# Moving sums to VectorE and block copies to ScalarE, decoding weights in slices of 768, and re-pricing the hand-written order of a delta-rule plus channel-mixer kernel

## The chip, the core and the metric

The kernel runs on one core of a Trainium2 chip. The metric is the device time of one execution in microseconds (us). Engines are called PE (TensorE, matrix products), DVE (VectorE), ACT (ScalarE), POOL (GpSimd) and SP (the engine that only issues DMAs here). PEld is PE's weight load.

## What is computed

Four batches, eight heads, 768 time steps, 48 dimensions per head. First a delta-rule recurrence runs over time, then its output `x` (768 x 384 per batch) goes through a mixer with a low-rank product over the sequence and two dense layers over the channels. The weights arrive as 64-bit floats, everything else as fp32.

```
k_n = k / (norm(k) + 1e-6)
for t in range(S):
    y[t]  = q[t] @ state
    v_old = state^T k_n[t]
    state = state + beta[t] * outer(k_n[t], v[t] - v_old)
x  = y as (B, S, 384)
u  = x + (x^T @ U @ V)^T                    # U 768x32, V 32x768
out = u + relu(u @ w_ch1) @ w_ch2           # w_ch1 384x1536, w_ch2 1536x384
```

## The kernel before

**Recurrence.** Time is cut into chunks of 64, six chunks make a unit, two units make a batch, so there are eight units n = 0..7 and two SBUF slots that they share in turn. For each unit `grams` transposes k and q on PE (L380), copies them on ACT (L395) and forms the products k·k and q·k (L407, masked on DVE at L431). `blocks` then inverts the triangular systems: DVE transposes the diagonal blocks of 32 (L481), runs a forward substitution of pairs of instructions `prod` (L490) and `xt` (L496), and transposes back (L503). With `split = 2` (units 0 to 3) a block of 32 is solved as two blocks of 16 in 15 steps, and `joins` puts the halves together with small PE products (L534, L551) and extra DVE work (L513, L559). With `split = 1` (units 4 to 7) there are 31 longer steps. The joined blocks of 64 are made by L581 to L602, the results negated and copied by L610 (ACT) and L613 (DVE), and the diagonal blocks are copied into the slot by L624 (POOL, 48 times) and L627 (ACT, 16 times); POOL also clears blocks (L631). `prepare` makes two more products (L704, L715), copied by L723 (ACT) and L728 (DVE). `recur` steps through the twelve chunks of a batch: PE products L753, L781, L668, L682, with the DVE instructions `z` (L766) and `s` (L791) between them and copies of the output into `X` on ACT (L652).

**Mixer.** `front` (L903, L917, L925) makes `ut`, the transposed u, for 256 time steps. `wide` first multiplies by w_ch1 (L990, 72 PE records, then the relu on ACT, L946), and then by w_ch2 (L1026, 84 records, added into `X` on DVE, L975). I call these two halves "wide" and "narrow"; there are twelve of each, three per batch. The narrow half uses seven products of half size in place of eight, which needs sums of hidden activations (`add_up` L962, `last_sum` L969, both on POOL) and of weights (`sums`, L815, POOL, eight instructions).

**Weights.** `load_weights` decodes 64-bit floats on the fly: a slice of 384 columns is loaded into `wide` through POOL's DMA queue (L835), and five DVE instructions (L852, L861, L867, L872, L880) with one of ACT (L857) turn it into fp32. There are 27 slices: U, two of V, twelve of w_ch1, twelve of w_ch2. The first wide half needs all of w_ch1, the first narrow half all of w_ch2 and the weight sums.

**Order.** Nothing is scheduled at run time. Each part is a generator that yields the engine and price of its next operation; `run` keeps one clock for each engine, and picks the next operation by place in a priority list and by modelled time. The order found in this way is the program's order on each engine[...]. A price in an `op(...)` call is therefore no time on the chip: it only moves instructions. `SWITCH` and `HOLD` are the model's charges for changing PE's kind of work and for holding back. For example:

```
yield op("pool", 1.2)
nc.gpsimd.tensor_tensor(out=w[:, to], in0=w[:, a], in1=w[:, c], op=ALU.subtract)
```

Of the kernel before, what the change touches and what calls it, by code (L numbers as in the profile page):

```python
# [26 lines left out]
def kernel(  # L27
# [36 lines left out]
    HD = DM // 2  # L64

# [17 lines left out]
    clock = dict(pe=0.8, dve=0.8, act=0.8, pool=0.8, sp=0.8)  # L83
# [4 lines left out]
    SWITCH, HOLD = 0.15, 0.15  # L88
# [8 lines left out]
    def op(engine, cost, mode=None, take=None, give=(), lat=None, rush=None, words=0):  # L97
        return dict(e=engine, cost=cost, mode=mode, take=take, give=give, words=words + 2,
                    rush=bool(give) if rush is None else rush, lat=LAT[engine] if lat is None else lat)
# [26 lines left out]
    def run():  # L126
        while waits:
            some = {}
            for i in sorted(waits):
                while isinstance(waits.get(i), list) and all(x in done for x in waits[i]):  # L130
                    at = max([0.0] + [done[x] for x in waits[i]])
                    if at > ready[i]:
                        last[i] = None
                    advance(i, None, max(at, ready[i]))
                s = waits.get(i)
                if s is None or isinstance(s, list):
                    continue
                e, was = s["e"], last.get(i)
                at = max(was[1] if was and was[0] == e else ready[i], clock[e])
                if s["take"]:  # L140
                    banks, of = places(s)
                    if not of:
                        continue
                    at = max(at, min(banks[y] for y in of))
                if s["mode"] and s["mode"] != state["mode"]:
                    at += SWITCH
                some.setdefault(e, []).append((at, i))
# [28 lines left out]
            state["now"] = clock[s["e"]] = at + cost  # L176
            if s["mode"]:
                state["mode"] = s["mode"]
# [87 lines left out]
    def load(n, name, halves):  # L266
# [13 lines left out]
        for g in halves:  # L280
            for s in range(1, 4, 2) if name == "z" else range(4):
                to = dict(k=s, q=s, v=s % 2 * 2 + s // 2, z=s // 2)[name]
                yield op(e, 0.65)
                queue.dma_start(
                    out=t[half(1 - g if name == "z" else g), :, to, 0:D],
                    in_=src[b, 4 * g + s, hf * UC * L : (hf + 1) * UC * L, :].rearrange(
                        "(c t) d -> t c d", t=L
                    ),
                )
                after = landing(384)  # L290
                if name == "z" or s % 2:
                    emitted((name, n, g, s // 2), after)
# [4 lines left out]
    def load_beta(u):  # L297
        beta_sb = X.rearrange("p a b d -> p (a b d)")[0 : 4 * B, 0 : 2 * S].rearrange(
            "p (g s) -> p g s", g=2
        )  # L300
        if u == 0:
            for g in range(2):
                yield op("pool", 0.6)
                nc.gpsimd.dma_start(out=beta_sb[:, g], in_=beta[:, 4 * g : 4 * g + 4])
            yield op("pool", 0.0, lat=landing(64, 0.1))
        else:
            yield need(("gram", 0))
# [30 lines left out]
    def norms(n):  # L338
# [9 lines left out]
        yield op("dve", 0.9)  # L348
# [24 lines left out]
    def grams(n, i):  # L373
# [26 lines left out]
        def products(j, i):  # L400
            yield need(("laid", n)) if i else []
            x = yield op("pe", 0.75, "Q", take="pair", words=96)
# [25 lines left out]
            else:  # L428
                for par in range(2):
                    yield op("dve", dve(384), give=[("pair", x)] if par else (), rush=n >= NU)  # L430
# [28 lines left out]
    def blocks(n):  # L459
        _, _, pg, _, _, _, diag, _ = units[n]  # L460
        split = 2 if n in (0, 1, 2, 3) else 1
# [18 lines left out]
        yield op("dve", dve(BK * BK))  # L480
# [3 lines left out]
        yield op("dve", dve(1024 // split))  # L484
        nc.vector.tensor_tensor(out=gb, in0=gb, in1=by, op=ALU.mult)
        for j in range(size - 1):
            m, w = j + 1, size - 1 - j
            yield op("dve", 2 * dve(split * m * w) - 0.08)
# [13 lines left out]
        yield op("dve", dve(BK * BK))  # L502
# [17 lines left out]
        def joins(r):  # L520
# [53 lines left out]
            for c in range(UC):  # L574
                if c % 3 == 0:
                    got = yield op("pe", 0.23, "J", take=None if c else "pair", words=48)
# [13 lines left out]
            for c in range(UC):  # L590
                if c % 3 == 0:
                    got = yield op("pe", 0.23, "J", take=None if c else "pair", words=48)
# [12 lines left out]
            for g in range(2):  # L605
                rows = quarter(2 * g)
                to = pg[rows, r, :, :, BK:L]
                if g == 0:
                    yield op("act", act(384), rush=True)
                    nc.scalar.mul(to, p_v[rows], -1.0)  # L610
                else:
                    yield op("dve", dve(384), give=[("pair", x)])
                    nc.vector.tensor_scalar_mul(to, p_v[rows], -1.0)  # L613
            emitted(("upper", n, r), 0.1)

        def diagonals(r):
            at = slice(12 * r, 12 * r + 12)
            yield need(("whole", n, r))
            for i in range(4):
                a = BK * (i % 2)  # L620
                to, of = heads(pg[quarter(i)])[:, at, a : a + BK], zc[quarter(i), at]
                if i < 2 or r == 0:
                    yield op("pool", 0.5)
                    nc.gpsimd.tensor_copy(out=to, in_=of)  # L624
                else:
                    yield op("act", act(384))
                    nc.scalar.copy(to, of)  # L627
# [12 lines left out]
    def recur(b):  # L640
# [19 lines left out]
        def outputs(c, s_old):  # L660
# [3 lines left out]
            y = yield op("pe", 0.35, "Q", take="pair", words=32)  # L664
            p_y = pair(y)[:, :, 0 : 2 * D]
            if c > 0:
# [11 lines left out]
                yield op("pe", 0.35, "Q", words=32)  # L678
# [16 lines left out]
        def prepare(n, h):  # L695
# [4 lines left out]
            x = yield op("pe", 0.76, "Q", take="pair", words=96)  # L700
# [10 lines left out]
            y = yield op("pe", 0.76, "Q", take="pair", words=96)  # L711
# [15 lines left out]
            yield op("dve", dve(576), give=[("pair", y)])  # L727
            nc.vector.tensor_copy(  # L728
# [10 lines left out]
        for c in range(NC):  # L739
# [9 lines left out]
            else:  # L749
                xb = yield op("pe", 0.35, "Q", take="pair", words=32)  # L750
# [24 lines left out]
            if c < NC - 1:  # L775
                yield need(("y1", b, c)) if c else []
                xs = yield op("pe", 0.35, "Q", take="pair", words=32)
# [18 lines left out]
    WIDE = 384  # L796

    def weight_slices():
        yield u_sb.rearrange("p c r -> p (c r)"), moe_U, NB
        for s0 in range(0, S, WIDE):  # L800
            yield v_sb[:, s0 : s0 + WIDE], moe_V[:, s0 : s0 + WIDE], None
        for f in (0, 2, 1, 3):
            for t in range(KT):
                at = slice(f * WIDE, (f + 1) * WIDE)
                yield w1_sb[:, t, at], moe_w_ch1[t * 128 : (t + 1) * 128, at], None
        for f in range(HF):
            yield w2_sb[:, 0:4:3, f], moe_w_ch2[f * 128 : (f + 1) * 128, :], None
            at = slice((HF + f) * 128, (HF + f + 1) * 128)
            yield w2_sb[:, 1:3, f], moe_w_ch2[at, :], None

    def sums(f):
        w = w2_sb[:, :, f : f + 3]
        for to, a, c in ((4, 3, 0), (5, 2, 4), (6, 1, 5), (3, 2, 3)):
            yield op("pool", 1.2)
            nc.gpsimd.tensor_tensor(out=w[:, to], in0=w[:, a], in1=w[:, c], op=ALU.subtract)  # L815
        emitted(("sums", f), 0.2)

    def load_weights():
        landed = {}
        slices = list(weight_slices())  # L820

        def start(i):
            dst, src, groups = slices[i]
            n = WIDE if len(dst.shape) == 3 else dst.shape[1]
            wide = conv.tile([128, n, 2], I32, name="wide")
            src = src.bitcast(I32)
            to = wide.rearrange("p n two -> p (n two)")
            copies = 1 if groups else 128 // src.shape[0]
            if groups:
                to = to.rearrange("p (c r) -> p c r", c=groups)  # L830
                src = src.rearrange("(c p) r -> p c r", c=groups)
            for x in range(copies):
                yield op("pool", 0.55)
                at = slice(x * 128 // copies, (x + 1) * 128 // copies)
                nc.gpsimd.dma_start(out=to[at], in_=src)  # L835
            landed[i] = wide
            emitted(("wide", i), landing(128, 0.13) + 0.6)
# [3 lines left out]
        for i in range(len(slices)):  # L841
            dst = slices[i][0]
            n = WIDE if len(dst.shape) == 3 else dst.shape[1]
# [3 lines left out]
            yield op("dve", 0.36)  # L847
            wide = landed.pop(i)
            h, low = wide[:, :, 1], wide[:, :, 0].bitcast(U32)
            power = conv.tile([128, n], I32, name="power", bufs=1)  # L850
            upper = conv.tile([128, n], I32, name="upper", bufs=1)
# [4 lines left out]
            yield op("act", 0.62, lat=-0.62)  # L856
# [3 lines left out]
            yield op("dve", 0.36)  # L860
# [5 lines left out]
            yield op("dve", 0.57)  # L866
# [4 lines left out]
            yield op("dve", 0.57)  # L871
# [4 lines left out]
            yield op("dve", 0.57)  # L876
            power = power.bitcast(FP32)
            if len(dst.shape) == 3:
# [5 lines left out]
            if i >= 3 + KT * DFF // WIDE and (i - 3 - KT * DFF // WIDE) % 6 == 5:  # L884
                begin(sums((i - 3 - KT * DFF // WIDE) // 6 * 3), 21)
# [7 lines left out]
    def front(b, i):  # L893
        yield need(
            ("front", *before(b, i)), ("wide", *before(*before(b, i))),
            ("weights", 2), *[("x", b, c) for c in range(NC)],
# [17 lines left out]
        def block(c):  # L914
            o = yield op("pe", 0.72, "F", take="pair", words=4)
# [6 lines left out]
            o = yield op("pe", 0.38, "F", take="pair", words=6)  # L922
# [12 lines left out]

    def wide(b, i):
        yield need(("front", b, i), ("narrow", *before(b, i)))
        x, ut = X[:, b % 2], uts[b, i]
        if b == 0 and i == 0:
            state["slow"] = 1.0  # L940
            yield op("pe", 0.0, take=("pair", 3))
            free["mix"].update({0: state["now"], 1: state["now"]})
# [10 lines left out]
        def add_up(f0, fs):  # L953
            yield need(*[("h", b, i, x) for x in fs])
            at = slice(f0, f0 + 3)
            for to, a, c, how in (
# [4 lines left out]
                yield op("pool", 0.8)  # L961
                nc.gpsimd.tensor_tensor(out=to, in0=a, in1=c, op=how)  # L962
            emitted(("summed", b, i, f0), 0.1)

        def last_sum():
            yield need(("summed", b, i, 0), ("summed", b, i, 3), ("half", b, i, 1))
            yield op("pool", 1.5)
            a = part(1, 0, 0, HF)
            nc.gpsimd.tensor_tensor(out=a, in0=a, in1=S2, op=ALU.subtract)  # L969
# [13 lines left out]
        for y, fs in enumerate(((0, 1), (2, 6), (7, 8), (3, 4), (5, 9), (10, 11))):  # L983
            for f in fs:
                yield need(("weights", 2 + KT * ((0, 2, 1, 3).index(f // 3) + 1)))
# [48 lines left out]
    with tc.manual_schedule():  # L1034
# [16 lines left out]
        begin(load_weights(), 40)  # L1051
        for b in range(B):
# [36 lines left out]
```

## Time and profile before

| what | value |
|---|---|
| median of 3 runs | 751.82 us (751.59 to 757.63) |
| the profiled execution | 749.14 us, span 747.4 us |
| PE busy | 621.5 us (83%) |
| DVE busy | 396.9 us (53%), 928 instructions |
| ACT busy | 183.5 us (25%), 369 instructions |
| POOL busy | 208.9 us (28%), 265 instructions |
| mean granted TensorE clock | 0.881 |
| twelve wide halves (L990) on PE | 205.2 us |
| twelve narrow halves (L1026) on PE | 179.9 us |
| substitution (L490 and L496) on DVE | 150.5 us |
| sums of activations on POOL (L962, L969) | 94.8 us |
| sums of weights on POOL (L815) | 11.6 us, eight instructions |

The span is the trace's own length; the profiled execution's time is 1.7 us above it. A busy share is an average over stages that differ: up to about 200 us the recurrence of batches 0 and 1 and the decoding of weights fill DVE, and from about 560 us on only the mixer is left and PE is always busy. The profile's chain of waits is followed back from the last instruction, so it shows what set the end and not only what was busy.

### The profile page before, as it was taken

Reading aid. Unit: us, or ns where it says so; the run is one execution under the profiler, and the core shown is the slowest. Engines: PE = TensorE matmul, PEld = TensorE weight load, DVE = VectorE, ACT = ScalarE, POOL = GpSimd, SP = SyncE. Lnnn points to the kernel's source line nnn. Section 1 sums busy time; section 2 is a strip of 40 time slices with the busy share of each in tenths; the row PEclk is TensorE's granted clock in tenths of the full one; section 3 lists DMA queues with packets and bytes.
Section 4 is the critical chain, followed back from the end, with each engine's and each line's share of the span. In section 5 each row is a group of like instructions: output and inputs, shape, how many; then the busy total and the mean of one; then the engine's idle time right before and its main releaser. Section 6 shows DMA issues by size and latency. Waiting matters only on the chain.

```text
span 747.4 us, 25030 instructions
## 1 busy us (share of the span) xinstructions
PE 621.5 (83%) x11304; PEld 539.9 (72%) x11304; DVE 396.9 (53%) x928; ACT 183.5 (25%) x369; POOL 208.9 (28%) x265
## 2 busy tenths in 40 slices
PE   5567677956698897876799587799999999999998
PEld 4556665745587676755778586688888989989998
DVE  6998788999832269989227989821110110101001
ACT  3232346422112343211226211222112011120110
POOL 7443311355212111322301231330213131221412
PEclk9555569965689999879999787999999999999999
DMA  9603657412002243000324200000000000000000
GB/s 154 97 19 91 144 146 170 104 42 68 2 4 53 55 72 69 27 3 2 58 52 90 52 13 13 3 2 23 3 22 1 22 0 22 11 11 22 1 22 22
DMA packets 87051, 33.38 MB, mean 45 GB/s; under 512 B 81760, under 2 KB 84832, under 8 KB 86944
## 3 DMA queue, kind: packets, MB, share of 16 engines
q1 hardware_dynamic: 81856, 19.18, 13.5%
q0 software_dynamic: 3488, 12.29, 6.2%
q8 instruction: 89, 1.46, 0.8%
q10 hardware_dynamic: 1600, 0.30, 0.2%
q14 instruction: 18, 0.15, 0.1%
HBM read 27.03 MB, written 4.72 MB: 42 GB/s over the span
## 4 chain that ended last, share of the span: by engine, by line
PE 42%; DVE 20%; issue 2%; ACT 2%; DVEq 0%
PE P L990 18%; PE P L1026 17%; DVE prod L490 6%; DVE xt L496 6%; DVE zz L503 1%; PE P L917 1%; DVE slot L431 1%; PE P L781 1%; PE P L753 1%; PE P L925 1%; DVE gs L481 1%; DVE z L766 1%; ACT X L652 1%; DVE slot L420 1%; DVE X L921 1%
## 5 line engine op out<-in xcount | busy, mean ns | idle before, releaser
L990 PE MATMUL P<-ut,w_sb 128*128 128x256 f32 x864 | 205.2, 391 | 3.6 <-ACT hs L946 3.6
L990 PEld LDWEIGHTS P<-ut,w_sb 128*128 128x128 f32 x864 | 163.3, 194 | 26.7 <-ACT hs L946 4.0
L1026 PE MATMUL P<-w_sb,hs 128*128 128x192 f32 x720 | 128.2, 335 | 0.5 <-DVE X L975 0.5
L1026 PEld LDWEIGHTS P<-w_sb,hs 128*128 128x128 f32 x720 | 120.5, 195 | 3.8 <-issue 1.2
L975 DVE TENSOR_TENSOR X<-X,P 128x192 f32<-128x192 f32 x84 | 29.6, 353 | 157.3 <-PE P L1026 157.2
L946 ACT ACTIVATE hs<-P 128x512 f32<-128x512 f32 x72 | 42.8, 596 | 226.5 <-PE P L990 212.1
L962 POOL TENSOR_TENSOR S<-hs 128x384 f32<-128x384 f32 x24 | 24.3, 1011 | 264.7 <-ACT hs L946 264.7
L490 DVE TENSOR_TENSOR prod<-gs,xt 128x30 f32<-128x30 f32 (+20 forms) x184 | 77.5, 421 | 4.4
L496 DVE TENSOR_TENSOR xt<-xt,prod 128x30 f32<-128x30 f32 (+20 forms) x184 | 73.0, 397 | 6.3
L652 ACT COPY X<-P 64x192 f32<-64x192 f32 x96 | 30.1, 314 | 93.0 <-PE P L682 71.8
L1026 PE MATMUL P<-w_sb,S 128*128 128x192 f32 x288 | 51.7, 336 | 0.0
L1026 PEld LDWEIGHTS P<-w_sb,S 128*128 128x128 f32 x288 | 48.7, 196 | 0.5
L407 PE MATMUL P<-slot 48*64 48x64 f32 x1536 | 36.6, 260 | 10.9 <-DVE slot L613 6.3
L407 PEld LDWEIGHTS P<-slot 48*64 48x64 f32 x1536 | 32.9, 171 | 15.3 <-DVE slot L613 6.4
L380 PE MATMUL P<-ident,slot 128*128 128x128 f32 x192 | 31.9, 315 | 11.0 <-DMA slot<-in_k_dram 7.0
L921 DVE TENSOR_TENSOR X<-X,P 128x384 f32<-128x384 f32 x24 | 12.7, 547 | 46.5 <-PE P L917 46.1
L624 POOL COPY slot<-zz 32x384 f32<-32x384 f32 x48 | 24.6, 512 | 40.1 <-DVE zz L559 38.2
L380 PEld LDWEIGHTS P<-ident,slot 128*128 128x128 f32 x192 | 25.0, 160 | 14.7 <-issue 13.5
L969 POOL TENSOR_TENSOR hs<-hs,S 128x768 f32<-128x768 f32 x12 | 22.0, 1829 | 41.5 <-PE P L1026 41.5
L766 DVE TENSOR_TENSOR z<-slot,P 128x192 f32<-128x192 f32 x44 | 15.5, 353 | 31.1 <-PE P L753 30.0
L925 PE MATMUL P<-ident,X 128*128 128x128 f32 x72 | 13.5, 312 | 20.5 <-DVE X L921 20.3
L363 POOL TENSOR_TENSOR slot<-slot,norm_rows 128x1152 f32<-128x1152 f32 x8 | 18.8, 2349 | 40.2 <-DMA slot<-in_q_dram 28.1
(108 smaller groups left out, 857.3 us busy)
## 6 DMA issues: line engine op xcount, KB each, us to landing
wide<-in_moe_w_ch_dram POOLq DMA_DIRECT2D x24, 384.0 KB, 3.9
slot<-in_k_dram SPq DMA_DIRECT2D x84, 72.0 KB, 3.3
slot<-in_q_dram SPq DMA_DIRECT2D x64, 72.0 KB, 3.3
out_dram<-X SPq DMA_DIRECT2D x24, 192.0 KB, 1.8
slot<-in_v_dram SPq DMA_DIRECT2D x48, 72.0 KB, 2.5
slot<-in_v_dram POOLq DMA_DIRECT2D x16, 72.0 KB, 4.3
wide<-in_moe_V_dram POOLq DMA_DIRECT2D x8, 96.0 KB, 5.5
slot<-in_k_dram POOLq DMA_DIRECT2D x8, 72.0 KB, 6.4
```

What stands on the lines that cost most here:

```text
L380: nc.tensor.transpose(p_t[:, c // 3, c % 3], t[:, c, 2 * j : 2 * j + 2].rearrange("p s d -> p (s d)"), ident,)
L407: nc.tensor.matmul(p_g[half(g ^ (par * i)), par, c], kq[rows, c, j, 0, half(g)], kq[rows, c, j, i, half(g)], start=True, stop=True,)
L490: nc.vector.tensor_tensor(out=prod, in0=gb[:, :, j : j + 1, j + 1 :].to_broadcast([128, split, m, w]), in1=xb[:, :, 0:m, j : j + 1].to_bro ...
L496: nc.vector.tensor_tensor(out=xb[:, :, 0:m, j + 1 :], in0=xb[:, :, 0:m, j + 1 :], in1=prod, op=ALU.subtract,)
L624: nc.gpsimd.tensor_copy(out=to, in_=of)
L652: nc.scalar.copy(x[half(c % 2), c // 2, 4 * D * g : 4 * D * (g + 1)].rearrange("p (j r d) -> p r j d", r=2, d=D), states(p_y)[half(g)],)
L766: nc.vector.tensor_tensor(out=z.rearrange("p (r j) d -> p r (j d)", r=2), in0=vn[:, cu].rearrange("p (r j) d -> p r (j d)", r=2), in1=p_b, ...
L946: nc.scalar.activation(hs[:, fs[0] : fs[1] + 1 : fs[1] - fs[0]], p_f, ACTF.Relu)
L962: nc.gpsimd.tensor_tensor(out=to, in0=a, in1=c, op=how)
L975: nc.vector.tensor_tensor(out=to, in0=to, in1=p, op=ALU.add)
L990: nc.tensor.matmul(p_f[:, fs.index(f)], w1_sb[:, t, f * 128 : (f + 1) * 128], ut[:, t], start=(t == 0), stop=(t == KT - 1),)
L1026: nc.tensor.matmul(p_o, a[:, f], w2_sb[:, w, f], start=(first and f == 0), stop=(f == HF - 1), skip_group_check=True,)
```

## The change

Six things are done at once.

1. All sums leave POOL for DVE: `sums` (eight instructions of 128x576), `add_up` (72 of 128x384) and `last_sum` (12 of 128x768).
2. Block copies leave POOL and DVE for ACT: all 64 diagonal copies, both negated copies (L613), and the copy after the product L715 (L728).
3. Weights are decoded in slices of 768 columns: U, one slice of V, six of w_ch1, six of w_ch2. Their loads go through SP's queue (that of U stays on POOL's). Half of the buffers lie in `X[:, 1]`, batch 1's part of `X`, which is not needed yet; beta's staging moves from `X` to `hs` for that.
4. Only units 0 and 1 are solved in blocks of 16; units 2 and 3 now use 31 steps.
5. The order model gets a `port` clock, shared by POOL's operations and by the DVE operations with `port=True`, and many prices change. This alters the order on every engine.
6. Two PSUM banks are reserved for the mixer by a part of its own (`reserve`).

```
-    clock = dict(pe=0.8, dve=0.8, act=0.8, pool=0.8, sp=0.8)
+    clock = dict(port=0.0, pe=0.8, dve=0.8, act=0.8, pool=0.8, sp=0.8)
-    SWITCH, HOLD = 0.15, 0.15
+    SWITCH, HOLD = 0.18, 0.18
...
+                if s["port"]:
+                    at = max(at, clock["port"])
...
+            if s["port"]:
+                clock["port"] = at + cost
...
-        split = 2 if n in (0, 1, 2, 3) else 1
+        split = 2 if n in (0, 1) else 1
...
-                if g == 0:
-                    yield op("act", act(384), rush=True)
-                    nc.scalar.mul(to, p_v[rows], -1.0)
-                else:
-                    yield op("dve", dve(384), give=[("pair", x)])
-                    nc.vector.tensor_scalar_mul(to, p_v[rows], -1.0)
+                yield op("act", act(384), rush=True, give=[("pair", x)] if g else ())
+                nc.scalar.mul(to, p_v[rows], -1.0)
...
-                if i < 2 or r == 0:
-                    yield op("pool", 0.5)
-                    nc.gpsimd.tensor_copy(out=to, in_=of)
-                else:
-                    yield op("act", act(384))
-                    nc.scalar.copy(to, of)
+                yield op("act", act(384))
+                nc.scalar.copy(to, of)
...
-            yield op("dve", dve(576), give=[("pair", y)])
-            nc.vector.tensor_copy(
+            yield op("act", act(576), give=[("pair", y)])
+            nc.scalar.copy(
                 out=vn[:, cs[0] : cs[2] + 1].rearrange("p c (r j) d -> p r c (j d)", r=2),
...
-    WIDE = 384
+    WIDE = 768
...
-            yield op("pool", 1.2)
-            nc.gpsimd.tensor_tensor(out=w[:, to], in0=w[:, a], in1=w[:, c], op=ALU.subtract)
+            yield op("dve", dve(576), port=True)
+            nc.vector.tensor_tensor(out=w[:, to], in0=w[:, a], in1=w[:, c], op=ALU.subtract)
...
+        room = X.bitcast(I32).rearrange("p a b d -> p a (b d)")[:, 1]
+        wides = [room[:, 0 : 2 * WIDE], conv.tile([128, 2 * WIDE], I32, name="wide", bufs=1)]
+        uppers, powers = room[:, 2 * WIDE :], conv.tile([128, WIDE], I32, name="power", bufs=1)
...
+            e, queue = ("pool", nc.gpsimd) if i < 1 else ("sp", nc.sync)
+            for to, of in pieces:
+                yield op(e, 0.6, port=False)
+                queue.dma_start(out=to, in_=of)
...
+    def reserve():
+
+        yield [("x", 0, NC - 2)]
+        yield op("pe", 0.0, take=("pair", 3))
+        free["mix"].update({0: state["now"], 1: state["now"]})
+        emitted("mixing")
...
-                yield op("pool", 0.8)
-                nc.gpsimd.tensor_tensor(out=to, in0=a, in1=c, op=how)
+                yield op("dve", dve(384), port=True)
+                nc.vector.tensor_tensor(out=to, in0=a, in1=c, op=how)
...
-            yield op("pool", 1.5)
+            yield op("dve", dve(768), port=True)
             a = part(1, 0, 0, HF)
-            nc.gpsimd.tensor_tensor(out=a, in0=a, in1=S2, op=ALU.subtract)
+            nc.vector.tensor_tensor(out=a, in0=a, in1=S2, op=ALU.subtract)
```

## The prediction

> **What bounds the kernel now.** I read the page's slices first. The rows are tenths of busy time in forty slices of 18.7 us.
>
> ```profile
> PE   5567677956698897876799587799999999999998
> DVE  6998788999832269989227989821110110101001
> PEclk9555569965689999879999787999999999999999
> ```
>
> DVE is full in the first ten slices while PE is half idle at a low clock; from slice 30 on PE is full. The page gives averages, so I cut the span at the ends of the recurrences of batches 0 to 3, which the timeline of L682 shows at 117, 265.5, 393 and 562.3 us. Busy time by stretch, with count in brackets:
>
> ```profile
> core 0: us, PE busy (x) PEld busy (x) DVE busy (x) ACT busy (x) POOL busy (x), PEclk, DMA share, GB/s
> 0.00:117.00 117.00, 77.77 (x2812) 69.08 (x2816) 96.64 (x244) 41.05 (x85) 49.63 (x88) 0.64 0.56 110
> 117.00:158.00 41.00, 33.39 (x379) 26.26 (x370) 36.97 (x76) 18.04 (x32) 14.61 (x15) 0.92 0.53 120
> 158.00:199.00 41.00, 21.43 (x890) 18.57 (x888) 38.87 (x80) 9.24 (x19) 18.69 (x22) 0.58 0.12 39
> 265.50:393.00 127.50, 102.88 (x2175) 86.19 (x2175) 90.46 (x209) 32.84 (x69) 30.27 (x38) 0.95 0.21 41
> 393.00:562.30 169.30, 146.54 (x2447) 125.41 (x2443) 94.03 (x220) 41.41 (x84) 38.76 (x44) 0.93 0.11 24
> 562.30:747.40 185.10, 181.36 (x968) 164.75 (x964) 19.87 (x51) 24.82 (x45) 46.27 (x42) 1.00 0.04 14
> ```
>
> From 158 to 199 DVE is busy 38.9 of 41 us and PE 21.4. The first wide half is done at 158, but the last weight slice is decoded at 189.2 (last L880) and the last L815 ends at 194.2, so the first L1026 starts at 200.5. That delay feeds the tail: 182 us of mixer are left when the last recurrence ends. The timeline shows why DVE is slow:
>
> ```profile
> 433.98 1.81 POOL L969 TENSOR_TENSOR hs<-hs,S 128x768 f32<-128x768 f32 x1 [12.13 <-PE P L1026]
> 434.21 1.77 DVE L490 TENSOR_TENSOR prod<-gs,xt 128x175 f32<-128x175 f32 x1
> 436.02 0.34 DVE L496 TENSOR_TENSOR xt<-xt,prod 128x175 f32<-128x175 f32 x1
> ```
>
> The same shape takes 0.34 us alone and 1.77 beside a POOL instruction, ending with it. Summed over all DVE instructions, time above the shortest of the same shape is 59 us, of which 37 lie on L490 and L496. Last, the chain's tail is pure PE:
>
> ```profile
> 575.45 13.65 PE P L1026 x84
> 589.11 15.54 PE P L990 x72
> 604.64 1.41 PE P L903 x12
> ```
>
> [...]
>
> **The work, moved and removed.** PE work changes by little, but its place changes much. I priced every PE instruction of both programs' orders by full-clock rows of the chain: wide 15.54 us, narrow 13.65, L917 0.325 each, six L380 0.67, L407 group 0.90, L704 0.86, L715 0.84, a recurrence group 0.45. Mixer + recurrence work in us, between the ends of the recurrences:
>
> | stage | before | elapsed before | after |
> |---|---|---|---|
> | A, to batch 0's end | 0+54 | 117 | 0+52 |
> | B, to batch 1's end | 45+50 = 95 | 148.5 | 93+45 = 138 |
> | C, to batch 2's end | 54+42 = 97 | 127.5 | 81+43 = 124 |
> | D, to batch 3's end | 95+44 = 139 | 169.3 | 78+42 = 120 |
> | E, the rest | 176 | 185.1 | 119 |
>
> So 57 us of mixer leave the tail and must fit into B, C and D. Whether they fit is the question.
>
> *Stage A.* Twelve chunk steps of waits between PE and DVE set it, not DVE's sum. DVE has 7 us less, ACT six copies of 0.51 us more per unit. Bounds −6 to +4; I take 0: **117**.
>
> *Stage B, DVE.* Adjacent starts give a queue cost of 0.47 us for a 384 operation (L867 to L872), 0.27 for L852, and 0.20 + n/960 for a substitution operation (192 elements: 0.40). A 768 slice is then 2 x 0.48 + 3 x 0.87 = 3.6 us, against 2 x 1.95 for two slices of 384: 0.3 us saved on each of 13. From `tt` (the former L909) to the last weight sum the new DVE order holds five slices 17.9, eight sums at 0.67 = 5.4, six activation sums 2.8, six X additions 2.8, eight L420 2.2, a transpose 1.9, norms 1.4, masks 0.9: 35 us. Loads add to it: between these points SP issues about 34 DMAs at 0.65 us = 22 us, with weight slices in line behind unit loads; the last slice is issued near 140, lands some 6 us later (384 KB took 3.9), and decode and sums behind it take 10. A slice that waits on SP for its buffer holds unit 2's and 3's loads behind it; unit 2's k follows the last w_ch1 slice, well before it is used, so I take 0 for that. With 4 for sharing: 160, that is 117 + 43; bounds 35 and 60. Behind it in DVE's queue stands unit 2's substitution. Thirty-one steps cost 2 x (31 x 0.20 + 5456/960) = 23.8 us against 2 x (15 x 0.20 + 1360/960) = 8.8 plus 1.9 of extra transposes and joins: 13 us more, twice. Unit 2: 23.8 + scale 1.2 + transpose 1.9 + mixer's L975 and sums 4.2 = 31. Unit 3: the same with transposes, masks, norms and ten recurrence operations: 40. Nine for waits on PE: unit 3 is solved at 117 + 43 + 31 + 40 + 9 = **240** (206 before). From there stage C before took 39 us (L503's end at 353.7 to 393) with seven mixer groups between; the new order has seven too. B ends at **279**, PE doing 138 of 162 us. The first narrow half starts at 160 rather than 200.5.
>
> *Stages C and D.* DVE's chain in C: 4 us of start, unit 4's list 38, unit 5's 40, the last 39: 121 us; D the same. PE work is 124 and 120. POOL keeps only the row scaling (2.35 us, once per unit) as a reader of SBUF. Since PE and DVE wait for each other in fixed orders, PE will not be full. D before had PE work of 139 in 169; without its 11.6 us of excess on DVE (trace, 400 to 500) that is 88%. I take 88%: 124/0.88 = 141, 120/0.88 = 136. Batch 3 ends at 279 + 141 + 136 = **556**.
>
> *Stage E.* 185.1 − 57 = 128, and one front less (1.2) against X additions that now queue behind 1.4 us of sums: **128**. Sums there are free, since DVE is busy 20 of 185 us[...].
>
> *ACT.* 48 copies at 0.51, 16 at 0.48, 16 at 0.64 (between 0.48 for 384 and 0.80 for 768) add 42 us to 183, of some 690: hidden, except one or two copies ahead of L589 per unit, within stage A's bound. Batch 1's first copy into `X`, near 200, comes after the decoding there has ended. The reservation of banks costs 0; both ways banks are free before the first wide half.
>
> Sum: 556 + 128 = 684 of span, +1.7 = 686 for the profiled execution, +2.7 as the median stood over it: **688**.
>
> **Rivals.**
> (1) *Full overlap.* PE at 95% in B to D: 382/0.95 = 402, 117 + 402 + 128 + 4.4 = 651. For it: stage E reaches 98%. Against: no stage with a recurrence passed 88%.
> (2) *Weights late, or the chains no shorter.* Weights come at +60, not +43, since slices wait on SP behind loads: 17 us, 705. Or C keeps its 127 and D its 169 because latencies and not PE set them: 279 + 296 + 128 + 4.4 = 707. For it: 28 unit loads share DMA with 3.8 MB of weights in 30 us. Against: D had 139 of PE work, now 120.
> (3) *DVE becomes the bound; slower.* Sums stand in DVE's order between substitution steps and wait there for PE, where before POOL waited (264.7 us, idle). Stages B to D hold 16 groups of L962's kind and eight of L969's. Slower by 1% needs 759 − 688 = 71 us, or 3.0 us of wait on the path at each of the 24. For it: DVE's total at the queue costs above rises 56 us (359 to 415). Against: most sums stand after relus long done.
> (4) *Nothing gained from the port:* DVE's own operations replace POOL's locks, 59 us of excess against 56 added. Then C and D stay as in (2), and it is no different in time.
>
> **How the numbers follow.** Main case 0.50 (its own range 670 to 703), (1) 0.18, (2) with (4) 0.26, (3) 0.06 of which half passes 759. The range 655 to 722 leaves out the outer part of (1), the worst of (2), and (3). One per cent is about what a measurement of this kernel can tell: faster 0.94, same 0.02, slower 0.04.
>
> **What would show it.** First narrow half near 160; unit 3's back-transpose near 240; recurrence ends near 117, 279, 420, 556; 128 us of tail; excess on L490 and L496 under 20 us. It would be wrong if DVE shows long idle times ahead of the sums with the substitution behind them, or if the last weight slice lands after 165.

## The result and the profile after

The changed kernel takes 667.45 us (median of 4 runs, 665.52 to 669.34), the kernel before 754.73 in the runs beside it. The ratio is 0.884, with a 95% interval of 0.879 to 0.890. The profiled execution took 667.06 us, of which 664.8 are span. In the lines that follow, the changed kernel's line numbers stand: L990 has become L1012, L1026 L1048, L490 and L496 are L498 and L504, L962 is L984.

The slices of the page, as shown for before (each is now 16.6 us):

```profile
PE   5678657688999999889899999998998999999998
DVE  6788647689999962499798225998781213121212
PEclk9556558979999999899999999997999999999999
```

From the ninth slice on no digit of PE is below 8; before, that held only from the 27th. But for single dips later, the low clock ends after nine slices, where it took twelve. DVE is still full or nearly so from the ninth to the fourteenth slice, but PE now runs beside it.

Busy time by stretch, cut at the ends of the four recurrences (113.3, 273.5, 406.2, 538.0 us) and at the first narrow half (163.5):

```profile
core 0: us, PE busy (x) PEld busy (x) DVE busy (x) ACT busy (x) POOL busy (x), PEclk, DMA share, GB/s
0.00:113.30 113.30, 75.09 (x2743) 66.79 (x2743) 82.52 (x197) 48.82 (x96) 31.11 (x54) 0.62 0.53 108
113.30:163.50 50.20, 39.62 (x449) 30.42 (x446) 38.79 (x63) 21.13 (x35) 2.20 (x1) 0.90 0.60 139
163.50:273.50 110.00, 105.81 (x2058) 92.86 (x2060) 81.25 (x208) 36.21 (x76) 9.10 (x13) 1.00 0.13 29
273.50:406.20 132.70, 127.83 (x2353) 105.56 (x2342) 90.11 (x226) 50.67 (x101) 10.98 (x14) 0.99 0.20 39
406.20:538.00 131.80, 125.46 (x2305) 107.62 (x2305) 86.48 (x224) 46.64 (x94) 9.34 (x11) 0.96 0.13 30
538.00:664.80 126.80, 123.14 (x654) 111.15 (x654) 29.80 (x63) 17.24 (x32) 0.00 (x0) 1.00 0.04 13
```

The tail is 126.8 us where it was 185.1. Batch 3's recurrence ends at 538.0 where it was 562.3, although 57 us more of mixer lie ahead of it. So 58 us came from the tail and 24 from the stages before it, together the 82.6 us by which the span fell.

What the order model calls the port, and the prediction locks, shows in the traces as DVE instructions that end with a POOL instruction beside them. In the timeline of the changed kernel:

```profile
204.56 3.21 POOL L371 TENSOR_TENSOR slot<-slot,norm_rows 128x1152 f32<-128x1152 f32 x1 [6.19 <-issue]
204.58 1.22 DVE L493 TENSOR_TENSOR gs<-gs,cp 128x1024 f32<-128x1024 f32 x1
205.83 1.99 DVE L498 TENSOR_TENSOR prod<-gs,xt 128x31 f32<-128x31 f32 x1
207.86 0.19 DVE L504 TENSOR_TENSOR xt<-xt,prod 128x31 f32<-128x31 f32 x1
```

L371, the row scaling, is the only instruction of this kind (two inputs in SBUF) that POOL keeps. L493, which starts beside it, takes 1.22 us where the six of its shape average 1.20, and it is L371 that is longer here, 3.21 us where the median of the eight is 2.17. The next one, L498, needs 1.99 us for a shape whose partner takes 0.19 and ends with the POOL instruction. Time of DVE instructions above the shortest of their shape in the two traces (the "excess" from here on): 62 us before, 24.5 after; on the substitution alone 37 and 6.5. (The prediction's 59 us used the shortest in the trace of before alone.)

Which POOL instructions made the 37 us can be read from the trace of before, by taking the substitution instructions that a POOL instruction outlasts: the sums (L815, L962, L969) account for 23 us, the row scaling L363 for 10.6, the copies L624 for 2.2. The row scaling stays on POOL, and yet only 4.6 us of its share are left in the changed kernel, so what it lost cannot come from a change of its own engine; it meets the substitution less often under the new order. The sums themselves take 0.55, 0.75 and 0.95 us on DVE (128x384, 128x576, 128x768), where they took 1.01, 1.46 and 1.83 on POOL.

### The profile page after: what moved, and what is told of

The parts are those of the page before. It is cut to its first block, busy times and chain, and to the rows that moved or that the text cites. A ratio compares the mean times of both kernels' runs of the same rounds, so it can differ in the third digit from the quotient of the medians.

```text
span 664.8 us, 23398 instructions
## 1 busy us (share of the span) xinstructions
PE 596.9 (90%) x10536; PEld 514.4 (77%) x10536; DVE 409.0 (62%) x979; ACT 220.7 (33%) x432; POOL 62.7 (9%) x93
## 4 chain that ended last, share of the span: by engine, by line
PE 67%; DVE 15%; issue 4%; ACT 2%; DMA 1%; SPq 1%; DVEq 0%; ACTq 0%
PE P L1048 23%; PE P L1012 22%; DVE xt L504 4%; DVE prod L498 3%; PE P L415 3%; PE P L753 2%; PE P L704 2%; PE P L715 2%; PE P L388 2%; PE P L668 2%; PE P L682 2%; PE P L781 1%; PE P L933 1%; DVE X L937 1%; PE P L941 1%
## 5 line engine op out<-in xcount | busy, mean ns | idle before, releaser
L1012 PE MATMUL P<-ut,w_sb 128*128 128x256 f32 x864 | 200.7, 386 | 0.0
L1012 PEld LDWEIGHTS P<-ut,w_sb 128*128 128x128 f32 x864 | 161.2, 191 | 22.6 <-issue 0.6
L1048 PE MATMUL P<-w_sb,hs 128*128 128x192 f32 x720 | 128.2, 333 | 0.0
L1048 PEld LDWEIGHTS P<-w_sb,hs 128*128 128x128 f32 x720 | 118.3, 193 | 1.4
L504 DVE TENSOR_TENSOR xt<-xt,prod 128x112 f32<-128x112 f32 (+21 forms) x216 | 73.2, 339 | 7.4
L498 DVE TENSOR_TENSOR prod<-gs,xt 128x112 f32<-128x112 f32 (+21 forms) x216 | 73.7, 341 | 5.1
L1048 PE MATMUL P<-w_sb,S 128*128 128x192 f32 x288 | 50.4, 330 | 0.1
L984 DVE TENSOR_TENSOR S<-hs 128x384 f32<-128x384 f32 x24 | 13.3, 555 | 57.1 <-ACT hs L968 57.0
L1048 PEld LDWEIGHTS P<-w_sb,S 128*128 128x128 f32 x288 | 46.7, 190 | 0.9 <-DVE X L997 0.4
L627 ACT COPY slot<-zz 32x384 f32<-32x384 f32 x64 | 32.6, 509 | 30.2 <-DVE zz L511 22.0
L415 PEld LDWEIGHTS P<-slot 48*64 48x64 f32 x1536 | 30.7, 160 | 10.1 <-issue 5.2
L766 DVE TENSOR_TENSOR z<-slot,P 128x192 f32<-128x192 f32 x44 | 15.5, 352 | 35.6 <-PE P L753 26.8
L403 ACT COPY slot<-P 128x768 f32<-128x768 f32 x30 | 23.8, 807 | 28.4 <-PE P L388 28.1
L371 POOL TENSOR_TENSOR slot<-slot,norm_rows 128x1152 f32<-128x1152 f32 x8 | 19.8, 2478 | 133.4 <-DVE norm_rows L368 49.9
L753 PEld LDWEIGHTS P<-s,slot 48*64 48x64 f32 x704 | 16.0, 147 | 15.3 <-issue 4.6
L753 PE MATMUL P<-s,slot 48*64 48x48 f32 x704 | 21.1, 238 | 7.4 <-DVE s L793 2.6
```

Source lines behind the costliest of these rows:

```text
L403: nc.scalar.copy(to, p_t)
L415: nc.tensor.matmul(p_g[half(g ^ (par * i)), par, c], kq[rows, c, j, 0, half(g)], kq[rows, c, j, i, half(g)], start=True, stop=True,)
L498: nc.vector.tensor_tensor(out=prod, in0=gb[:, :, j : j + 1, j + 1 :].to_broadcast([128, split, m, w]), in1=xb[:, :, 0:m, j : j + 1].to_bro ...
L504: nc.vector.tensor_tensor(out=xb[:, :, 0:m, j + 1 :], in0=xb[:, :, 0:m, j + 1 :], in1=prod, op=ALU.subtract,)
L753: nc.tensor.matmul(states(p_b)[half(g ^ par), par, j], kq[half(par, D), cu, j, 0, half(g)], states(s_old)[half(par, D), g, j], start=True, ...
L1012: nc.tensor.matmul(p_f[:, fs.index(f)], w1_sb[:, t, f * 128 : (f + 1) * 128], ut[:, t], start=(t == 0), stop=(t == KT - 1),)
```

## Experiments

Two numbers read every run: where the recurrences end, and how much mixer its program puts ahead of batch 3's end. The second is counted in the order of PE's instructions and priced as in the prediction, without the small transposes L925; it is known before a kernel runs. The same count made from the traces agrees within 1 us in all of them.

Small differences need care. The median of the kernel before moved by 1.9 us between the sets of runs (753.8 to 755.7). The ratio of the changed kernel, 0.879 to 0.890, overlaps with those of four of the runs that lie 2 to 5.5 us above it, so differences of this size are at the edge of what four executions tell. The stage times come from one profiled execution each, which can lie some us off the median.

| kernel | mixer in B, C, D, tail (us) | recurrence ends (us) | median (us) |
|---|---|---|---|
| before | 45, 54, 95, 176 | 117, 266, 393, 562 | 754.7 |
| changed | 93, 81, 78, 119 | 113, 274, 406, 538 | 667.5 |
| sums_on_pool | 93, 79, 80, 119 | 114, 287, 421, 553 | 680.2 |
| sums_on_pool_order_kept | as changed | 113, 278, 413, 545 | 673.0 |
| copies_back | 93, 77, 82, 119 | 112, 277, 409, 540 | 671.3 |
| four_units_split | 66, 86, 73, 146 | 116, 273, 420, 542 | 693.7 |
| order_model_as_before | 69, 64, 68, 171 | 121, 258, 387, 513 | 698.3 |
| weights_as_before | 93, 89, 78, 112 | 114, 298, 440, 563 | 682.1 |
| slices_768_pool_queue | as changed | 119, 281, 413, 545 | 671.7 |
| scaling_on_dve | 93, 93, 93, 93 | 117, 289, 432, 580 | 689.1 |
| scaling_dve_order_kept | as changed | 113, 276, 409, 543 | 669.4 |
| before_sums_copies_moved | 56, 74, 69, 173 | 119, 270, 404, 528 | 711.0 |
| before_moved_order_kept | as before | 118, 258, 383, 549 | 738.6 |
| before_two_units_split | 60, 62, 73, 176 | 123, 283, 420, 558 | 743.6 |

### The sums, with and without their order

**sums_on_pool**

```
-            yield op("dve", dve(576), port=True)
-            nc.vector.tensor_tensor(out=w[:, to], in0=w[:, a], in1=w[:, c], op=ALU.subtract)
+            yield op("pool", 1.2)
+            nc.gpsimd.tensor_tensor(out=w[:, to], in0=w[:, a], in1=w[:, c], op=ALU.subtract)
...
-                yield op("dve", dve(384), port=True)
-                nc.vector.tensor_tensor(out=to, in0=a, in1=c, op=how)
+                yield op("pool", 0.8)
+                nc.gpsimd.tensor_tensor(out=to, in0=a, in1=c, op=how)
...
-            yield op("dve", dve(768), port=True)
+            yield op("pool", 1.5)
             a = part(1, 0, 0, HF)
-            nc.vector.tensor_tensor(out=a, in0=a, in1=S2, op=ALU.subtract)
+            nc.gpsimd.tensor_tensor(out=a, in0=a, in1=S2, op=ALU.subtract)
```

> The changed kernel with all sums (weights, activations, last sum) back on POOL, priced for the order model as they were before; everything else as changed. Theory P ([...]POOL instructions with two SBUF inputs stop the substitution, so the sums cost DVE about as much from POOL as on it, but at worse places): 10 to 25 us slower than the changed kernel, 677 to 692, with the excess of the substitution instructions over their shortest time back from 6 to 20 us or more. Rival D (the sums load DVE, which the change pays for elsewhere): 5 to 15 us faster than the changed kernel, 652 to 662. Rival W (the gain is the early weights alone): within 5 us of 667.

680.2 us (ratio to before 0.898, 0.892 to 0.904), 12.7 slower than the changed kernel: theory P's band. The excess on the substitution rises from 6.5 to 34.5 us, all but back to before. Mixer placement hardly differs, and the tail is equal; the time is lost before batch 3's end (553 against 538).

**sums_on_pool_order_kept**: the same engines, but the three `yield op("dve", ...)` lines stay.

> As the run before, but the order model is told the prices of DVE, so that the order of all other instructions on PE, ACT, SP and DVE stays as in the changed kernel and only the engine of the sums differs. Theory P: 10 to 25 us slower than 667, since the locks are in the engine and not in the order. If the order is what mattered (rival O), this one is within 5 us of 667 while the run with POOL's prices is slower. Rival D: 5 to 15 us faster.

673.0 us (0.889, 0.884 to 0.895), 5.5 slower. That is below P's 10 to 25 and at the edge of O's 5, so neither expectation was clearly right. Excess on the substitution is 31 us, so the locks are there and DVE instructions last 27 us longer in all (52 against 24.5). DVE is also freed of 57 us of sums, and is busy 24 us less than in the changed kernel (385.1 against 409.0); yet the run is not faster. Less work on DVE did not pay here, with the stretch lying on the substitution. Taking the 5.5 as it stands, about 5 of the 12.7 us are the engine's and about 7 the order's that goes with the prices.

### The copies

**copies_back**

```
-                yield op("act", act(384))
-                nc.scalar.copy(to, of)
+                if i < 2 or r == 0:
+                    yield op("pool", 0.5)
+                    nc.gpsimd.tensor_copy(out=to, in_=of)
+                else:
+                    yield op("act", act(384))
+                    nc.scalar.copy(to, of)
...
-            yield op("act", act(576), give=[("pair", y)])
-            nc.scalar.copy(
+            yield op("dve", dve(576), give=[("pair", y)])
+            nc.vector.tensor_copy(
```

(and the second negated copy back on DVE)

> The changed kernel with the block copies back where they were: 48 diagonal copies on POOL, half of the negated copies and the copy after the second product of prepare on DVE. Theory P: these copies read SBUF on POOL (48 x 0.51 us) while DVE substitutes or decodes, and 16 x 0.55 + 16 x 0.75 us return to DVE: 8 to 20 us slower, 675 to 687. Rival A (ACT's longer queue on the way from the substitution to the recurrence costs as much as the port gives): within 5 us of 667.

671.3 us (0.886, 0.881 to 0.891), 3.9 slower: rival A's band, though nothing here shows A's reason. The DVE excess did not rise at all (24.3 against 24.5). The trace shows why. In that of before, a substitution instruction beside a POOL copy of 0.5 us ends 0.04 to 0.07 us after the copy (last section); here only three are outlasted by one of the 48 copies, and become 0.2 to 0.3 us longer each. The copies run when DVE is mostly past its substitution. DVE is busy 20 us more than in the changed kernel (429.4 against 409.0), and about 4 of these reach the end.

### The blocks of 16

**four_units_split**

```
-        split = 2 if n in (0, 1) else 1
+        split = 2 if n in (0, 1, 2, 3) else 1
```

> The changed kernel with units 2 and 3 also solved in blocks of 16. My estimate was 13 us of DVE less per unit, 26 in all, in the stage to batch 1's end. Theory P, with DVE as the setting engine there: batch 1's recurrence ends 10 to 20 us earlier and the total is 5 to 15 us faster, 652 to 662. Rival J (the joins' PE and ACT steps, in series between substitution and recurrence, cost what DVE gains): within 5 us of 667, or slower.

693.7 us (0.918, 0.912 to 0.924): 26 us slower, against both theories' main numbers, on the side that rival J allowed. Unit 3 was solved (end of its transpose back, L511) at 201.9 us and not at 237.5, earlier as the DVE sum said, but batch 1's recurrence ended at 273.2, as in the changed kernel. Stretches of this kernel, and then of the changed one:

```profile
164.90:200.00 35.10, 30.76 (x806) 27.79 (x808) 32.68 (x94) 8.51 (x19) 4.95 (x6) 0.76 0.04 14
200.00:240.00 40.00, 37.28 (x1142) 29.95 (x1135) 10.34 (x22) 15.20 (x34) 2.94 (x6) 0.78 0.18 33
240.00:273.20 33.20, 31.21 (x727) 27.25 (x726) 9.38 (x24) 9.99 (x22) 0.32 (x1) 0.95 0.16 35
```

```profile
163.50:200.00 36.50, 35.99 (x375) 33.09 (x373) 33.88 (x88) 8.69 (x18) 2.62 (x5) 1.00 0.03 12
200.00:240.00 40.00, 40.00 (x768) 33.36 (x763) 37.30 (x96) 12.80 (x29) 5.02 (x4) 1.00 0.09 21
```

The DVE column shows that DVE is mostly free from 200 us on with four split units, while PE is busy 68.5 of 73.2 us: PE takes over as the bound. It has more small instructions (1142 records against 768 from 200 to 240 us) and up to 240 us a granted clock of 0.76 to 0.78 where the changed kernel has 1.00. The joins of units 2 and 3 (L542 and L559, 768 records) alone keep PE busy for 10.8 us, which is rival J's mechanism as far as PE goes. The order of this kernel has 27 us less mixer in stage B, and these 27 us reappear in the tail (155.0 us, 542.3 to 697.3, against 126.8). Of the 32.5 us between the two spans 28.2 are the tail's and 4.3 come before it.

**before_two_units_split**: the same line, the other way, in the kernel before.

> The kernel before with only units 0 and 1 in blocks of 16. Its order still leaves 176 us of mixer for the tail. Theory S (in the changed kernel this part paid through the 27 us of mixer that it brought ahead, not by itself): within 12 us of the kernel before, or slower, since DVE has 26 us more where it is full. Rival J (longer substitutions are better by themselves, fewer joins on PE and ACT): 15 to 30 us faster.

743.6 us (0.984, 0.979 to 0.989): 10 us faster than before, inside theory S's band. Its tail of mixer stays at 176 us. So this part is worth 10 us alone and 26 in the changed kernel. Where the 10 us come from is not shown.

### The order model

**order_model_as_before** (core of the edit)

```
-                if s["port"]:
-                    at = max(at, clock["port"])
...
-    SWITCH, HOLD = 0.18, 0.18
+    SWITCH, HOLD = 0.15, 0.15
...
-                yield op("pe", 0.24, "Q", words=32)
+                yield op("pe", 0.35, "Q", words=32)
...
-        begin(reserve(), 0)
```

> The changed kernel's operations and engines, with the order model of before: no port clock, old prices for PE's groups, the transposes and the substitution, old SWITCH and HOLD, banks reserved where they were. In its order only 200 us of mixer stand ahead of batch 3's end and 171 after it (the changed kernel: 251 and 119; the kernel before: 195 and 176). Theory S (what counts is how much mixer the fixed order puts ahead of batch 3's end, where PE would else wait): the tail is about 179 us and the total 685 to 700. Rival P (the moved operations give the gain whatever the order): within 8 us of 667.

698.3 us (0.926, 0.921 to 0.931), in theory S's band; rival P falls. Batch 3's recurrence even ends 25 us earlier than in the changed kernel (513 against 538), but 171 us of mixer are left, and the tail takes 180 (513.0 to 692.9). Which of the model's edits does it was not tried one by one.

**before_sums_copies_moved**: sums on DVE, copies on ACT, in the kernel before, with prices `dve(576)`, `dve(384)`, `dve(768)` and `act(384)`, `act(576)`; no other part of the change.

> The kernel before with two parts of the change alone: sums on DVE and block copies on ACT. Four units in blocks of 16, slices of 384 on POOL's queue and the order model stay as before; its order leaves 172 us of mixer for the tail. Theory S with the port: the stages with recurrences get shorter by the lost excess (59 to some 20 us) but the tail stays at 181: 690 to 720. Rival P (the moved operations are the whole gain): 660 to 675. Rival N (sums on DVE cost what the port gives): 740 to 760.

711.0 us (0.943, 0.939 to 0.948): 43 us faster, in theory S's band. The tail of mixer stays (173), and batch 3's recurrence ends 34 us earlier. The last weight slice is decoded from 164.5 us on and no longer from 189.2, although the slices are still of 384 on POOL's queue: an earlier end of the decoding is not the large slices' alone.

**before_moved_order_kept**: the same engines, but `yield op("pool", ...)` and the other prices left as they were.

> The kernel before with sums on DVE and block copies on ACT, but the order model is told the old engines and prices, so that the order on PE is that of the kernel before (mixer 45, 54, 95 and a tail of 176 us). It separates the engines from the order in the run at 711. Theory P (locks gone): 20 to 40 us faster than the kernel before, 714 to 734, with an excess of DVE under 35 us instead of 62. Rival O (the order made the 43 us): within 10 us of the kernel before.

738.6 us (0.977, 0.972 to 0.983): 15 us faster, between the two expectations. Excess fell from 62 to 33 us, as P said, but the sums came to DVE, which is busy as long as before (397.6 against 396.9 us); under the old order 15 us reach the end. The other 28 us of the run at 711 come with the order that the same prices make.

### The weights

**weights_as_before**: `weight_slices` and `load_weights` of before (slices of 384, POOL's queue, own buffers) in the changed kernel.

> The changed kernel with the weights decoded in slices of 384 and loaded by POOL's queue, as before; sums, copies, units and order model as changed. Its order leaves 112 us of mixer for the tail, much like the changed kernel's 119. Theory S with my estimate of 0.3 us saved per 768 columns: 3 to 10 us slower than 667, that is 670 to 677. Rival W (big slices on SP's queue are what brings the first narrow half forward): first narrow half 15 us or more later than 163.5, total above 682.

682.1 us (0.905, 0.901 to 0.910), 14.6 slower, more than S's estimate and at the edge of rival W's total. W's sign did not come by the letter: the first narrow half starts early, at 153.7. In substance it did, since PE then waits for the decoding. The placement is as good (112 in the tail), so this one is a true delay. PE rows (L1032 is the narrow product in this kernel), idle time before each in brackets:

```profile
156.81 0.59 PE L1032 MATMUL P<-w_sb,hs 128*128 128x192 f32 x2 [2.25 <-DVE w_sb L880]
165.66 1.01 PE L1032 MATMUL P<-w_sb,hs 128*128 128x192 f32 x2 [8.26 <-DVE w_sb L880]
173.36 1.01 PE L1032 MATMUL P<-w_sb,hs 128*128 128x192 f32 x2 [6.69 <-DVE w_sb L880]
181.16 4.85 PE L1032 MATMUL P<-w_sb,hs 128*128 128x192 f32 x14 [6.80 <-DVE w_sb L880]
```

These are 24 us of waits for L880, whose last one starts at 183.6 (158.1 in the changed kernel). Batch 1's recurrence ends 24 us later. DVE is busy 8 us more (417.0 against 409.0), twice the prediction's 0.3 us for each of 13 slices. The run puts back slice size, queue, buffers and the order that comes of them together.

**slices_768_pool_queue**

```
-            e, queue = ("pool", nc.gpsimd) if i < 1 else ("sp", nc.sync)
+            e, queue = "pool", nc.gpsimd
```

> The changed kernel with all slices of 768 loaded by POOL's DMA queue; its mixer placement is that of the changed kernel. Theory S ([...]slice size and the order around it made the 15 us of the run with the old weights): within 5 us of 667, first narrow half within 5 us of 163.5. Rival Q (SP's queue made them): 675 or more.

671.7 us (0.890, 0.885 to 0.895), 4.3 slower: rival Q falls. The queue accounts for some 4 us at most, in the trace mainly in stage A (119 against 113); what they consist of is not shown. If the two add up, the slice size with buffers and order around it accounts for the other 10. The first narrow half began 8 us earlier, not within 5.

### One step further

**scaling_on_dve**

```
-        yield op("pool", 2.2)
-        nc.gpsimd.tensor_tensor(
+        yield op("dve", dve(1152), port=True)
+        nc.vector.tensor_tensor(
             out=vn.rearrange("p c (r j) d -> p r c j d", r=2),
```

> The changed kernel with POOL's last reader of SBUF, the row scaling of v (eight of 128x1152, some 2.4 us each on POOL), also on DVE (some 1.3 us each). Its order spreads the mixer evenly: 92.7 us in each of B, C, D and the tail. Theory S with the port: batch 3's end later, tail about 100 us, total 655 to 668; excess on the substitution near 2 us. Rival D (DVE sets the stages): 10 us of DVE more, total 672 to 680.

689.1 us (0.916, 0.910 to 0.922), 22 slower. The 1.3 us for each scaling is an estimate that fits L493, which at 128x1024 averages 1.20 us on DVE in the changed kernel. The excess of this run on the substitution is 1.9 us, as expected, and its mixer is spread evenly, which theory S should have liked. Theory S fails here: placement is not enough. Stages C and D of this kernel:

```profile
289.00:431.90 142.90, 139.71 (x2378) 118.67 (x2373) 93.29 (x233) 49.79 (x99) 5.88 (x12) 0.98 0.19 38
431.90:580.40 148.50, 140.04 (x2432) 120.44 (x2432) 94.39 (x235) 50.00 (x101) 4.27 (x9) 0.98 0.12 27
```

Twenty-seven us more of mixer were put into C and D, and C and D became 27 us longer (142.9 and 148.5 us against 132.7 and 131.8), while the tail shrank by only 22. PE was busy there 96 and 95% of the time in the changed kernel, and had hardly any room. So bringing mixer ahead paid only as far as PE stood idle there. The rest of the loss, 15.5 us, lies in stages A and B, where the count is the same: stage B took 172 us against 160, and after 240 us PE is busy 39.5 of 49 us at a granted clock of 0.75.

**scaling_dve_order_kept**: DVE executes, the model is told POOL's price.

> As the run with the row scaling on DVE, but the order model is told POOL's price, so that all engines keep the changed kernel's order and mixer placement (93, 81, 78, 119). Theory S (in the earlier run the new order cost the 22 us, not the scaling): within 6 us of 667. Rival D (ten us more on DVE cost it): 680 or more.

669.4 us (0.886, 0.881 to 0.891), not told apart from the changed kernel. So no cost of the scaling itself can be seen, and the new order cost the 20 us. For C and D the trace points to PE, as said above; why that order is worse in stage B was not settled. No version beat the changed kernel.

## Why the prediction was right

688 us was forecast with a range of 655 to 722; 667.5 was measured. By its own steps, in us of span:

| step | forecast | measured |
|---|---|---|
| A | 117 | 113.3 |
| first narrow half | 160 | 163.5 |
| unit 3 solved (end of its transpose back) | 240 | 237.5 |
| B, length | 162 | 160.2 |
| C | 141 | 132.7 |
| D | 136 | 131.8 |
| E | 128 | 126.8 |
| span | 684 | 664.8 |

*The placement of the mixer.* The count of PE's order decided the forecast, and it held: the tail fell by 58 us, counted as 57. The run with the same operations and engines and another order (698), the one with four split units (693.7) and the one with old order and new engines (738.6) support it. Their tails follow the count. But scaling_on_dve shows that the count gives only the tail; the length of the stages before it must be had in another way. There the question that the prediction left open, whether the 57 us fit into B, C and D, was answered by PE's idle time: it was enough for these 57 us and not for 27 more.

*The term that was off.* Of the 19 us of error, 12.5 lie in C and D, 3.7 in A. I took 88% of PE for C and D from stage D of before. With the counted work and the measured times it is 124/132.7 = 93% and 120/131.8 = 91%. That 88% came out of a single stage of before, which ran under the old order and whose excess on DVE I had only subtracted. The true share lies between it and the 95% of the rival "full overlap"; what raised it was not separated. The forecast is above the measured length in each of the five stages, so no stage makes good for another. In stage A, the bounds of −6 to +4 held.

*Stage B.* The length was right in part by luck. From batch 0's end to the first narrow half I counted 43 us, from there to unit 3's solution 80, and from there to the end 39; measured are 50, 74 and 36. The error of +7 is undone by −6 and −3. The 160 for the first narrow half was near only because stage A ended earlier than I said.

The reason was not complete either. I let unit 3's solution on DVE plus 39 us set batch 1's end. The changed kernel fits it (237.5 + 36.0 = 273.5), and the last weight loads were issued at 142.5 and 143.2 us where I said near 140. Yet in four_units_split unit 3 came 36 us earlier and the end stayed at 273.2. DVE and PE both bound stage B, and freeing one shows the other. My price of 13 us of DVE per unsplit unit stood in the sum as a cost, 26 us for two units (unit 3's solution moves by 36, waits included). Undoing it made the kernel slower and not faster: the joins are back on PE, and 27 us of mixer go back to the tail.

*The port.* Excess on the substitution was to be under 20 us and is 6.5. DVE's busy time rose by only 12 us (396.9 to 409.0): 57 us of sums and 28 us of longer substitution came, but 38 us of excess and 21 us of copies left, and the decoding and the joins became shorter. The rival "nothing gained from the port" was half right: with the order kept, moving the sums back costs some 5.5 us, no more.

*The other rivals.* "DVE becomes the bound" did not come: in stage E DVE is busy 29.8 of 126.8 us, and PE 123.1. "Weights late" came in part: the first narrow half starts 50 us after batch 0's end, between the 43 of the main case and the 60 of the rival, while the last L880 starts at 158.1, and PE waits for no weights after the first narrow half has begun. "The chains no shorter" gave 127 for C and 169 for D: C is indeed no shorter (132.7, with 27 us more of mixer), D is 37 us shorter.

*How the 87 us divide.* Undone one at a time in the changed kernel, the parts cost 12.7 (sums), 3.9 (copies), 26.2 (split), 14.6 (weights) and 30.8 us (order model). That these add to 88.2 proves no independence: sums and copies gave 43 us alone in the kernel before, while undone here one by one they cost 17 together, and the split 10 and 26.

## What to carry to other kernels

In a kernel with a fixed order and one engine-bound tail, count how much of the tail's work the new order puts ahead of the last dependency; that count gave the tail's time before anything ran, here 7 to 12 us under the measured tail. Work brought ahead paid here only where PE, the tail's engine, stood idle ahead of that dependency; with PE busy 96 and 95% in C and D, as in the changed kernel, another 27 us made the two stages 27 us longer. The count doesn't give the stages before it, so price those from the busiest engine's share in a stage of like work, and let both ends of that share into the range. When work moves between engines, run it once with the order kept: in the three pairs here the engine made 15 us, some 5 and nothing that could be told, the order 28, some 7 and, for the worse, 20. Neither can be read from the other.

## What was not expected of the hardware

*Which POOL instructions stop DVE.* The prediction shows the stop beside one sum; the trace of before tells which other POOL instructions make it. Substitution instructions beside a POOL tensor_tensor were longer by up to 1.96 us (six that L363 outlasts, 1.77 on average). Beside the memsets L631 they were not (eight, 0.02 at most). The copies L624 have one input and touch 32 partitions only, and beside them too the substitution is longer, by 0.21 to 0.38 us. A copy, then a memset, each with the substitution instruction beside it:

```profile
40.66 0.50 POOL L624 COPY slot<-zz 32x384 f32<-32x384 f32 x1
40.68 0.55 DVE L490 TENSOR_TENSOR prod<-gs,xt 128x56 f32<-128x56 f32 x1
```

```profile
41.79 0.41 POOL L631 MEMSET slot<- 32x384 f32 x1
41.83 0.24 DVE L490 TENSOR_TENSOR prod<-gs,xt 128x78 f32<-128x78 f32 x1
```

The shortest L490 of 128x56 takes 0.17 us; beside the copy it takes 0.55. The shortest of 128x78 takes 0.23; beside the memset it takes 0.24. All seven substitution instructions that a copy outlasts end 0.04 to 0.07 us after it. They are longer by 0.32 us on average, less than beside the sums, because a copy lasts only 0.5 us. Those that a sum outlasts (25, L815, L962 and L969) end 0.07 to 0.28 us after it. For copies and sums alike the delay in this trace is thus about what was left of the POOL instruction.

*PE's clock and small matmuls.* From 200 to 240 us four_units_split had PE busy 37.3 of 40 us at a granted clock of 0.78, the changed kernel 40.0 at 1.00. The former has 1142 records in that time, 384 of them joins of 32x16, the changed kernel 768 and none of these. So PE was granted 0.78 while its records show it busy 93% of the time; what decides the clock these runs do not show.
